# Adjacent score groups, column halves of the second query/key chunk, and sums in another tiling, in a two-layer attention and gated-MLP kernel on one core

## The chip, the cores and the metric

One core of one Trainium2 chip runs the whole program. The metric is the device time of one execution in microseconds (us), quoted as the median of the fast runs. A ratio of two kernels is the mean time of the one kernel's fast runs over the mean of the other's from the same rounds, so it is not quite the ratio of the medians.

## The reference

The sequence has 2048 tokens of width 512. Two attention blocks and two gated-MLP blocks alternate. The changed part is the attention block. It goes through 64 segments of 32 tokens one after the other. Each segment puts 8 memory rows in front, projects q, k and v for 32 heads of 128, and attends over the 40 rows. The first 8 rows of its output are the memory of the next segment, so the segments form a serial chain.

```python
n_seg = S // seg_len                       # 2048 / 32 = 64
mask = (idx[:, None] < M) | (idx[:, None] >= idx[None, :])
mem = mem0
for s in range(n_seg):
    h = jnp.concatenate([mem, xs], axis=1)             # 8 + 32 rows
    q = jnp.einsum('btd,dhe->bhte', h, Wq)             # k, v likewise
    scores = jnp.where(mask, jnp.einsum('bhqe,bhke->bhqk', q, k) * scale, -1e9)
    o = jnp.einsum('bhte,hed->btd', einsum('bhqk,bhke->bhqe', softmax(scores), v), Wo)
    mem = o[:, :M, :]
    outs.append(o[:, M:, :])
# ... x = x + attention(layernorm(x)); x = x + gated_mlp(layernorm(x)); both twice
```

## The kernel before

TensorE does one segment as a fixed stream of stages: q0, k0, q1, k1 (the two chunks of q and k), scores of group 0, v0, a filler, scores of group 1, v1, a filler, the sums of the memory rows (psM), the product with v (psO), the other sums (psD), a filler, the output projection (pw), a filler. The fillers are pieces of work that does not depend on the running segment (keys and values of the next block of rows, "psb", or a late part of the output projection, "pwB"). They cover the time in which VectorE and ScalarE work on the memory rows.

A projection chunk is 16 matmuls of 512 columns, in four column groups of 32. Each matmul carries its own weight load. `halved` says how many of the 16 are issued as two matmuls of 256 columns: the same columns, in more instructions.

```python
PE_PAGE = 256
SEGMENT_PE = 600
FILL_AHEAD = ((0, 0, 0, 106), (0, 0, 0, 94))
# ... cut
def mm_chunk(ps, lhs, rhs, kts=range(KT), halved=0):
    for kt in kts:
        for cg in range(4):
            k, r = 4 * kt + cg, rhs(kt, cg)
            n = halved * (k + 1) // 16 - halved * k // 16
            # ... n: this matmul in two parts of 256 columns, else one of 512
            for a, (o, r) in enumerate(parts):
                nc.tensor.matmul(o, lhsT=lhs(kt, cg), rhs=r, ..., tile_position=(0, 32 * cg))
# ... cut
def fills_of(s):                     # instructions (matmuls and weight loads) of the four fillers
    # ...
    if s % 4 == 0:
        return (2, 2, 4, 8) if s // 4 > 3 else (0, 0, 0, 0)
    return (8, 8, 16, 32) if s // 4 + 1 < NB else (0, 0, 0, 0)

def pads_of(s):                      # how many matmuls of each chunk are halved
    n = (3 * PE_PAGE - SEGMENT_PE - fills_of(s - 1)[3] - sum(fills_of(s)[:3]) + 1) // 2
    pads = dict.fromkeys(("q0", "k0", "q1", "k1", "v0", "v1"), 0)
    for chunk, most in (("v0", 16), ("k1", 16), ("v1", 16 if s % 4 == 0 else 8), ("q1", 12), ...):
        k = min(n, most - pads[chunk])
        pads[chunk] += k
        n -= k
    assert n == 0
    return pads
# ... cut: the order of one segment
r0 = qk(0); r2 = qk(2); qk_T(0, r0); r1 = qk(1); qk_T(2, r2); r3 = qk(3); qk_T(1, r1)
psS = att.tile([P, 2, 512], F32, name="psS")
scores(0)
qk_T(3, r3)
v_mm(0, psV[0][:, 0, :]); fill(); close(0)
scores(1); close(1)
v_mm(1, psV[1][:, 0, :]); fill()
# ... psM from onesG over 128 rows, pv(0), pv(1), psD, fill, Ln and Exp of psM, pw, fill
```

`pads_of` keeps every segment at 3 * 256 = 768 TensorE instructions, matmuls and weight loads counted together. It does so by issuing columns in more instructions than they need.

The softmax here doesn't subtract the row's maximum and nothing guards it: scores larger than these inputs give would overflow.

## Time and profile before

| | us |
|---|---|
| time, median of 3 runs | 1853.05 (1849.69 to 1855.57) |
| the two attention blocks, first to last q0 | 721.3 and 718.8 |
| one segment with a key/value filler, most of them | 11.16 |
| TensorE busy, VectorE busy, ScalarE busy | 1749.7, 1155.0, 1111.5 |

Two more lines of the same profile belong here. The first is from the page's table of DMA queues; its columns are packets, megabytes and the share of 16 engines' time.

```profile
q8 instruction: 400, 6.55, 1.5%
```

The page calls the kind of this queue "instruction". A packet is 6.55 MB / 400 = 16 KiB. TensorE has 51,152 matmuls and 51,176 weight loads, together 102,328, and 102,328 / 400 = 255.8. From these counts I take the packets for TensorE's instructions in pages of 256. They come during the whole of block 0, one every 3.81 us on average.

The second is from the waits of the weight loads (what was waited for: us in all, times, longest).

```profile
PEld L544 <- issue: 27.5, 59, 4.3
```

"issue" is idle time for which the profile shows no semaphore that was waited for. L544 is the matmul of the projection chunks.

### The profile page before, as it was taken

The numbers are of one execution on the slowest core, as the hardware profiler recorded it, in microseconds if no ns is written. First come the engines' busy times: TensorE is split into PE (matmuls) and PEld (weight loads), VectorE is DVE, ScalarE is ACT, GpSimd is POOL, SyncE is SP. The second block draws the span as 40 slices with busy tenths as digits, with TensorE's granted clock in tenths as the row PEclk, the third lists the DMA queues.
The fourth block names the chain that finished last, engine by engine and source line by source line (L and its number), as shares of the span: only waits on it lengthen the run. The fifth ranks groups of instructions, "written<-read, shape, count | busy, mean of one in ns | idle before, by whom it ended". The sixth has DMA issues, their size and how long they took to land.

```text
span 1848.6 us, 109448 instructions
## 1 busy us (share of the span) xinstructions
PE 1749.7 (95%) x51152; PEld 1246.7 (67%) x51176; DVE 1155.0 (62%) x2700; ACT 1111.5 (60%) x2074; POOL 137.1 (7%) x289
## 2 busy tenths in 40 slices
PE   2999999999999999889989999999999999998898
PEld 1777777777777777645547777777777777775455
DVE  1666666677667766584346666666766676665622
ACT  1667777767777766471036667677776777665500
POOL 5000000000000000032010000000000000003000
PEclk8999999999999999999999999999999999999999
DMA  9100000021002111268940000001200121125585
GB/s 347 54 20 19 20 20 21 21 71 41 20 20 82 35 30 34 88 157 172 201 134 22 23 22 22 22 22 45 82 25 23 48 86 26 35 62 150 113 174 131
DMA packets 189327, 126.78 MB, mean 69 GB/s; under 512 B 135896, under 2 KB 164328, under 8 KB 188872
## 3 DMA queue, kind: packets, MB, share of 16 engines
q1 hardware_dynamic: 167016, 71.01, 16.6%
q0 software_dynamic: 10560, 34.07, 5.6%
q10 hardware_dynamic: 11296, 14.70, 2.7%
q8 instruction: 400, 6.55, 1.5%
q14 instruction: 55, 0.45, 0.1%
HBM read 59.29 MB, written 33.56 MB: 50 GB/s over the span
## 4 chain that ended last, share of the span: by engine, by line
PE 86%; DMA 4%; DVE 4%; issue 3%; ACT 2%; POOL 1%; SPq 0%; ACTq 0%; POOLq 0%; DVEq 0%
PE psm L544 24%; PE psV L544 13%; PE pw L599 12%; PE psb L544 10%; PE pg L332 7%; PE psS L722 5%; PE psO L745 4%; PE pwB L611 3%; PE py L360 2%; PE psD L797 2%; PE pz L266 1%; PE psM L787 1%; DMA uT<-u 1%; DMA Wo_sb<-in_A_Wo_dram 1%; PE psM L788 1%
## 5 line engine op out<-in xcount | busy, mean ns | idle before, releaser
L544 PEld LDWEIGHTS <-hA 128*32 128x32 bf16 x19868 | 542.2, 96 | 167.7 <-DVE hA L655 51.6
L701 ACT CAST rows<-psm 128x512 bf16<-128x512 f32 x512 | 300.2, 586 | 197.8 <-PE psm L544 197.8
L544 PE MATMUL psm<-Wq_sb,hA 128*32 128x256 bf16 (+1 forms) x5768 | 274.4, 319 | 11.2 <-DVE hA L655 9.5
L599 PEld LDWEIGHTS <-uT 128*32 128x32 bf16 x16640 | 236.1, 97 | 59.9 <-DVE uT L807 49.8
L599 PE MATMUL pw<-Wo_sb,uT 128*32 128x128 bf16 x16640 | 262.5, 220 | 14.6 <-DVE uT L807 6.3
L544 PE MATMUL psm<-Wk_sb,hA 128*32 128x256 bf16 (+1 forms) x6623 | 275.0, 298 | 1.4 <-issue 0.7
L544 PE MATMUL psV<-Wv_sb,hA 128*32 128x256 bf16 x7477 | 274.7, 284 | 1.1 <-issue 1.0
L705 DVE STREAM_TRANSPOSE QQ<-rows 128x512 bf16<-128x512 bf16 x256 | 182.0, 711 | 77.9 <-ACT rows L701 76.7
L726 ACT ACTIVATE E<-psS 128x448 bf16<-128x448 f32 x256 | 140.0, 547 | 121.8 <-PE psS L722 121.8
L757 DVE TENSOR_TENSOR uT<-psO,Rt 128x384 bf16<-128x384 f32 x256 | 138.6, 541 | 119.3 <-ACT Rt L813 119.0
L705 DVE STREAM_TRANSPOSE KA<-rows 128x512 bf16<-128x512 bf16 x256 | 181.7, 710 | 43.5 <-ACT rows L701 43.2
L807 DVE TENSOR_TENSOR uT<-psO,Rm 128x128 bf16<-128x128 f32 x256 | 62.5, 286 | 169.5 <-PE psD L797 169.5
L813 ACT ACTIVATE Rt<-Rt 128x512 f32<-128x512 f32 x256 | 157.4, 629 | 4.1
L332 PE MATMUL pg<-z2n,wspT 128*128 128x344 bf16 x1024 | 156.1, 311 | 1.0 <-DVE u L340 1.0
L332 PEld LDWEIGHTS <-wspT 128*128 128x128 bf16 x1024 | 98.4, 98 | 55.4 <-issue 8.2
L805 ACT ACTIVATE Rt<-psD 128x1024 f32<-128x1024 f32 x128 | 131.2, 1025 | 6.0
L544 PEld LDWEIGHTS <-hB 128*32 128x32 bf16 x3072 | 88.4, 97 | 68.4 <-DVE hB L559 25.2
L722 PEld LDWEIGHTS <-KA 128*64 128x64 bf16 x2048 | 79.8, 113 | 67.1 <-DVE KA L705 40.4
L729 DVE TENSOR_TENSOR E<-E,maskN 128x448 bf16<-128x448 bf16 x256 | 95.2, 372 | 45.7 <-ACT E L726 45.7
L544 PE MATMUL psb<-Wq_sb,hB 128*32 128x512 bf16 x1024 | 92.1, 390 | 26.2 <-DVE hB L559 26.2
L782 ACT CAST VA<-psV 128x512 bf16<-128x512 f32 x128 | 75.0, 586 | 62.7 <-PE psV L544 62.7
L722 PE MATMUL psS<-QQ,KA 128*64 128x80 bf16 x2048 | 110.1, 208 | 1.9 <-issue 0.9
(147 smaller groups left out, 2219.4 us busy)
## 6 DMA issues: line engine op xcount, KB each, us to landing
Wo_sb<-in_A_Wo_dram POOLq DMA_DIRECT2D x8, 1024.0 KB, 13.5
xs<-xd ACTq DMA_DIRECT2D x32, 256.0 KB
o_d<-o_sb SPq DMA_DIRECT2D x126, 64.0 KB
y_o<-o_d SPq DMA_DIRECT2D x24, 256.0 KB
xd<-y_o SPq DMA_DIRECT2D x22, 256.0 KB
Wq_sb<-in_A_Wq_dram POOLq DMA_DIRECT2D x8, 512.0 KB, 7.2
Wk_sb<-in_A_Wk_dram POOLq DMA_DIRECT2D x8, 512.0 KB, 11.1
Wv_sb<-in_A_Wv_dram POOLq DMA_DIRECT2D x8, 512.0 KB, 11.5
```

What stands on the lines that cost most here:

```text
L332: nc.tensor.matmul(pg[t][:, k, 0:344], lhsT=wsp[t][:, st, :], rhs=z2n[:, st, 344 * k:344 * k + 344], start=(st == 0), stop=(st == NT - 1))
L544: nc.tensor.matmul(o, lhsT=lhs(kt, cg), rhs=r, start=(kt == 0 and a == 0), stop=(kt == KT - 1 or halved > 0), tile_position=(0, 32 * cg), ...
L599: nc.tensor.matmul(po[32 * cg:32 * cg + 32, 0:128], lhsT=lhs[:, n, :], rhs=wo_rhs(h, cg), start=(h == 0), stop=(h == H - 1), tile_position ...
L701: nc.scalar.copy(r[:], ps[:])
L705: nc.vector.transpose(out=QQ[:, j % 2, :, 0:32] if j < 2 else KA[:, j % 2], in_=r[:])
L722: nc.tensor.matmul(pS[64 * g:64 * g + 64, i, c0:80 if K is KA else 112], lhsT=K[:, r, n:n + 2, :].rearrange("p h k -> p (h k)"), rhs=q if ...
L726: nc.scalar.activation(out=E[:, r], in_=pS, func=ACT.Exp, scale=scale)
L729: nc.vector.tensor_tensor(out=E[:, r], in0=E[:, r], in1=maskN[:, j4, :].unsqueeze(1).to_broadcast([P, 4, 112]), op=ALU.mult)
L757: nc.vector.tensor_tensor(out=hview(uT_nxt[:], r, 8, 32), in0=oview(r, 8, 32), in1=Rr[:, :, :, 0:24], op=ALU.mult)
L782: nc.scalar.copy(VA[:, 1].rearrange("p i e -> p (i e)"), psV[1][:, 0, :])
L805: nc.scalar.activation(out=Rt[:], in_=psD[:], func=ACT.Ln)
L813: nc.scalar.activation(out=rt, in_=rt, func=ACT.Exp, scale=-1.0)
```

## The change

The intent is to take changes of tiling and waits out of a segment. The scores of both groups go next to each other. The second chunk of q and of k is computed in two column halves, each in a bank (a buffer that matmuls write into) of its own, so that its copies and transposes can start earlier. The memory-row sums use the tiling of the product with v that follows. The late part of the output projection, used as a filler, is issued in column groups so that it has the tiling of its neighbours. `pads_of` is rewritten too: the halves put 2 x 16 = 32 more matmuls into a segment, and as many are taken out of the other chunks, so a segment keeps its 768 instructions.

```diff
@@ wo_last (the late part of the output projection, a filler)
+            w = P // parts
             for h in heads:
-                nc.tensor.matmul(pwB[:], lhsT=oBs[G][:, n, :], rhs=..., start=..., stop=...)
+                for t in range(0, P, w):
+                    nc.tensor.matmul(pwB[t:t + w, :], lhsT=oBs[G][:, n, t:t + w], rhs=..., tile_position=(0, t))
@@ fills_of
-                return (2, 2, 4, 8) if s // 4 > 3 else (0, 0, 0, 0)
+                return (8, 8, 16, 32) if s // 4 > 3 else (0, 0, 0, 0)
@@ pads_of
-            pads = dict.fromkeys(("q0", "k0", "q1", "k1", "v0", "v1"), 0)
-            for chunk, most in (("v0", 16), ("k1", 16), ("v1", 16 if s % 4 == 0 else 8), ("q1", 12), ("k0", 8), ...):
+            pads = dict(q0=0, k0=0, q1=16, k1=16, v0=0, v1=0)
+            n -= 32
+            for chunk, most in (("k0", 8), ("v0", 8), ("v1", 8), ("v0", 16), ("k0", 16), ("v1", 16), ("q0", 16)):
@@ segment
+            def qk_halves(j):
+                r = rowp.tile([P, 512], BF16, name="rows", tag="rowsQK", bufs=4)
+                for a in range(2):
+                    ps = ((att, attO[1]), (attO[0], accB))[j // 2][a].tile([P, 512], F32, name="psm2")
+                    # 16 matmuls of 256 columns into ps[:, 0:256]
+                    nc.scalar.copy(r[:, 256 * a:256 * a + 256], ps[:, 0:256])
+                    yield
+                    nc.vector.transpose(out=out, in_=r[:, 256 * a:256 * a + 256])
 ...
-            r1 = qk(1)
             qk_T(2, r2)
-            r3 = qk(3)
-            qk_T(1, r1)
-            scores(0)
-            qk_T(3, r3)
-            v_mm(0, psV[0][:, 0, :])
+            q1, k1 = qk_halves(1), qk_halves(3)
+            for g in (q1, q1, k1, q1, k1, k1):
+                next(g, None)
+            v_mm(0, psV)
+            pS = [scores(r) for r in range(2)]
+            # exps and masks of both groups
+            v_mm(1, psW)
             fill()
-            scores(1)
-            v_mm(1, psV[1][:, 0, :])
             fill()
 ...
-            for g in range(2):
-                o = psM[:, 128 * g:128 * g + 128]
-                nc.tensor.matmul(o, lhsT=onesG[:, g, :], rhs=a_part(0, P, 0, 2, 0, 8), ...)
-                nc.tensor.matmul(o, lhsT=onesG[:, g, :], rhs=b_part(0, P, 0, 2, 0, 8), ...)
+            for part in (a_part, b_part):
+                for g in range(2):
+                    nc.tensor.matmul(psM[:, g, 0:128], lhsT=ones[64 * g:64 * g + 64, :],
+                                     rhs=part(64 * g, 64 * g + 64, 0, 2, 0, 8), ...)
             pv(0)
-            pv(1)
             # ... psD
+            # Ln and Exp of psM
+            psO.append(attO[1].tile([P, 2, 512], F32, name="psO"))     # psM's banks
+            pv(1)
             fill()
```

Cut here: the second filler of a segment gets another bank, and the multiplication of the last rows moves behind the transpose that feeds the next segment.

More of the change, by code (lines that the diff above doesn't have):

```diff
@@ L573, in b_units @@
             for k, j in enumerate((0, 2, 1, 3, 4, 5)):
-                ps = (accA if k % 2 == 0 or not early else accB).tile([P, 512], F32, name="psb")
+                if early or k % 2 == 0:
+                    ps = (accA if k % 2 == 0 else accB).tile([P, 512], F32, name="psb")[:]
+                else:
+                    ps = att.tile([P, 512], F32, name="psb2")[:]
                 for kts in (((0,), (1,), (2, 3)), ((0, 1, 2, 3),))[k % 2]:
@@ L582, in out @@
                     if j >= 4:
-                        nc.scalar.copy(bs["VB"][:, j - 4].rearrange("p i e -> p (i e)"), ps[:])
+                        nc.scalar.copy(bs["VB"][:, j - 4].rearrange("p i e -> p (i e)"), ps)
                         return
                     r = rowp.tile([P, 512], BF16, name="rowsB", bufs=2)
-                    nc.scalar.copy(r[:], ps[:])
+                    nc.scalar.copy(r[:], ps)
                     turns.append(lambda: nc.vector.transpose(
@@ L605, in store_last, with wo_last @@
             eng.dma_start(o_d[M + 512 * G:M + 512 * G + 512, :].rearrange("(j r) d -> j r d", r=32)[:, 24:32, :], yB.pop(G)[:])
-        def wo_last(G, heads, pwB):
+        def wo_last(G, heads, pwB, parts=1):
+            w = P // parts
             for h in heads:
                 n = h // 8 * 8 + 2 * (h % 4) + h // 4 % 2
-                nc.tensor.matmul(pwB[:], lhsT=oBs[G][:, n, :], rhs=Wo_sb[:, h, :].rearrange("p (kt g el) -> p g kt el", kt=4, g=4),
-                                 start=(h == heads[0]), stop=(h == heads[-1]))
+                for t in range(0, P, w):
+                    nc.tensor.matmul(pwB[t:t + w, :], lhsT=oBs[G][:, n, t:t + w], rhs=Wo_sb[:, h, :].rearrange("p (kt g el) -> p g kt el", kt=4, g=4),
+                                     start=(h == heads[0]), stop=(h == heads[-1]), tile_position=(0, t))
                 yield
@@ L617, in y_part @@
             pwB = accA.tile([P, DM], F32, name="pwB")
-            for k, _ in enumerate(wo_last(G, range(8 * q, 8 * q + 8), pwB)):
+            for k, _ in enumerate(wo_last(G, range(8 * q, 8 * q + 8), pwB, 4)):
                 if k in (0, 1, 3):
@@ L673, in pads_of @@
             n = (3 * PE_PAGE - SEGMENT_PE - fills_of(s - 1)[3] - sum(fills_of(s)[:3]) + 1) // 2
-            pads = dict.fromkeys(("q0", "k0", "q1", "k1", "v0", "v1"), 0)
-            for chunk, most in (("v0", 16), ("k1", 16), ("v1", 16 if s % 4 == 0 else 8), ("q1", 12), ("k0", 8), ("q1", 16), ("v1", 16),
-                                ("k0", 16), ("q0", 16)):
+            pads = dict(q0=0, k0=0, q1=16, k1=16, v0=0, v1=0)
+            n -= 32
+            for chunk, most in (("k0", 8), ("v0", 8), ("v1", 8), ("v0", 16), ("k0", 16), ("v1", 16), ("q0", 16)):
                 k = min(n, most - pads[chunk])
@@ L705, in qk_T @@
                 nc.vector.transpose(out=QQ[:, j % 2, :, 0:32] if j < 2 else KA[:, j % 2], in_=r[:])
+            def qk_halves(j):
+                r = rowp.tile([P, 512], BF16, name="rows", tag="rowsQK", bufs=4)
+                for a in range(2):
+                    ps = ((att, attO[1]), (attO[0], accB))[j // 2][a].tile([P, 512], F32, name="psm2")
+                    for kt in range(KT):
+                        for cg in range(4):
+                            nc.tensor.matmul(ps[32 * cg:32 * cg + 32, 0:256].rearrange("p (i c) -> p i c", i=2), lhsT=hA_cur[:, kt, :],
+                                             rhs=qk_rhs(j, kt, cg)[:, 2 * a:2 * a + 2], start=(kt == 0), stop=(kt == KT - 1),
+                                             tile_position=(0, 32 * cg))
+                    nc.scalar.copy(r[:, 256 * a:256 * a + 256], ps[:, 0:256])
+                    yield
+                    out = (QQ[:, 1, :, 0:32] if j < 2 else KA[:, 1])[:, 8 * a:8 * a + 8]
+                    nc.vector.transpose(out=out, in_=r[:, 256 * a:256 * a + 256])
             def v_mm(r, ps):
@@ L714, in scores @@
             def scores(r):
-                pS = psS[:, r, 0:448].rearrange("p (i c) -> p i c", i=4)
+                psS = (att, attO[0])[r].tile([P, 512], F32, name="psS")
+                pS = psS[:, 0:448].rearrange("p (i c) -> p i c", i=4)
                 for i in range(4):
@@ L725, in scores, with exps @@
                                              start=(i == 0 and K is KA), stop=True, tile_position=(0, 64 * g), skip_group_check=True)
+                return pS
+            def exps(r, pS):
                 nc.scalar.activation(out=E[:, r], in_=pS, func=ACT.Exp, scale=scale)
@@ L753, in hview, with r_view, last_out @@
                 return t.rearrange("p (b n) q -> p b n q", b=4)[:, 2 * r:2 * r + 2, :, lo:hi]
+            def r_view(r):
+                return Rt[:].rearrange("p g (r n q) -> p g r n q", r=2, n=8)[:, :, r]
             def tok_out(r):
-                Rr = Rt[:].rearrange("p g (r n q) -> p g r n q", r=2, n=8)[:, :, r]
                 nc.vector.tensor_tensor(out=hview(uT_nxt[:], r, 8, 32), in0=oview(r, 8, 32),
-                                        in1=Rr[:, :, :, 0:24], op=ALU.mult)
+                                        in1=r_view(r)[:, :, :, 0:24], op=ALU.mult)
+            def last_out(r):
                 nc.vector.tensor_tensor(out=hview(oB, r, 8 * (s % 16), 8 * (s % 16) + 8), in0=oview(r, 32, 40),
-                                        in1=Rr[:, :, :, 24:32], op=ALU.mult)
+                                        in1=r_view(r)[:, :, :, 24:32], op=ALU.mult)
             r0 = qk(0)
@@ L764, in segment @@
             qk_T(0, r0)
-            r1 = qk(1)
             qk_T(2, r2)
-            r3 = qk(3)
-            qk_T(1, r1)
-            psS = att.tile([P, 2, 512], F32, name="psS")
-            scores(0)
-            qk_T(3, r3)
-            psV = [attO[r].tile([P, 2, 512], F32, name="psV") for r in range(2)]
-            v_mm(0, psV[0][:, 0, :])
-            fill()
-            close(0)
-            nc.vector.tensor_copy(VA[:, 0].rearrange("p i e -> p (i e)"), psV[0][:, 0, :])
-            scores(1)
@@ L778, in segment @@
-            close(1)
-            spare1()
-            v_mm(1, psV[1][:, 0, :])
-            fill()
-            nc.scalar.copy(VA[:, 1].rearrange("p i e -> p (i e)"), psV[1][:, 0, :])
-            psM = accB.tile([P, 512], F32, name="psM")
-            for g in range(2):
-                o = psM[:, 128 * g:128 * g + 128]
-                nc.tensor.matmul(o, lhsT=onesG[:, g, :], rhs=a_part(0, P, 0, 2, 0, 8), start=(g == 0), stop=True, skip_group_check=True)
-                nc.tensor.matmul(o, lhsT=onesG[:, g, :], rhs=b_part(0, P, 0, 2, 0, 8), start=False, stop=True, skip_group_check=True)
@@ L789, in segment @@
-            psO = [attO[r].tile([P, 2, 512], F32, name="psO") for r in range(2)]
+            q1, k1 = qk_halves(1), qk_halves(3)
+            for g in (q1, q1, k1, q1, k1, k1):
+                next(g, None)
+            psV = attO[1].tile([P, 512], F32, name="psV")
+            v_mm(0, psV)
+            nc.vector.tensor_copy(VA[:, 0].rearrange("p i e -> p (i e)"), psV[:])
+            pS = [scores(r) for r in range(2)]
+            for r in range(2):
+                exps(r, pS[r])
+            for r in range(2):
+                close(r)
@@ new lines, in segment @@
+            spare1()
+            psW = accB.tile([P, 512], F32, name="psV")
+            v_mm(1, psW)
+            fill()
+            fill()
+            nc.scalar.copy(VA[:, 1].rearrange("p i e -> p (i e)"), psW[:])
+            psM = attO[1].tile([P, 2, 512], F32, name="psM")
+            for part in (a_part, b_part):
+                for g in range(2):
+                    nc.tensor.matmul(psM[:, g, 0:128], lhsT=ones[64 * g:64 * g + 64, :], rhs=part(64 * g, 64 * g + 64, 0, 2, 0, 8),
+                                     start=(part is a_part), stop=True, skip_group_check=True)
@@ L790, in segment @@
+            psO = [attO[0].tile([P, 2, 512], F32, name="psO")]
             psD = att.tile([P, 2, 512], F32, name="psD")
             pv(0)
-            pv(1)
             for part, q0, q1, c0 in ((a_part, 8, 40, 0), (b_part, 8, 16, 24)):
@@ L798, in segment @@
                                          start=(part is a_part and r == 0), stop=True, skip_group_check=True)
+            Rm = segp.tile([P, 2, 2, 64], F32, name="Rm", bufs=1)
+            rm = Rm[:].rearrange("p g r c -> p g (r c)")
+            nc.scalar.activation(out=rm, in_=psM[:, :, 0:128], func=ACT.Ln)
+            nc.scalar.activation(out=rm, in_=rm, func=ACT.Exp, scale=-1.0)
+            psO.append(attO[1].tile([P, 2, 512], F32, name="psO"))
+            pv(1)
             fill()
-            Rm = segp.tile([P, 2, 2, 64], F32, name="Rm", bufs=1)
-            rm = Rm[:].rearrange("p g r c -> p (g r c)")
-            nc.scalar.activation(out=rm, in_=psM[:, 0:256], func=ACT.Ln)
-            nc.scalar.activation(out=rm, in_=rm, func=ACT.Exp, scale=-1.0)
             Rt = segp.tile([P, 2, 512], F32, name="Rt", bufs=1)
@@ L819, in segment @@
                 build_hA(s + 1, pw)
+            last_out(0)
             if s > 0:
@@ L825, in segment @@
             tok_out(1)
+            last_out(1)
             run(turns)
```

## The prediction

> **What bounds the kernel now.** The page comes first: busy shares, then the chain that ended last. They say TensorE.
>
> ```profile
> PE 1749.7 (95%) x51152; PEld 1246.7 (67%) x51176; DVE 1155.0 (62%) x2700; ACT 1111.5 (60%) x2074; POOL 137.1 (7%) x289
> ...
> PE 86%; DMA 4%; DVE 4%; issue 3%; ACT 2%; POOL 1%; SPq 0%; ACTq 0%; POOLq 0%; DVEq 0%
> ```
>
> A busy share of 95% does not say that every microsecond is matmul streaming[...]. So I read the timeline of one attention segment, TensorE alone; columns are start, time until the group's end, engine, line, operation, tiles, count. There are 128 such segments (64 in each of two attention blocks), in about 1430 of the 1849 us.
>
> ```profile
> 304.74 1.05 PE L544 MATMUL psm<-Wq_sb,hA 128*32 128x512 bf16 x16
> ...
> 307.34 1.07 PE L544 MATMUL psm<-Wk_sb,hA 128*32 128x256 bf16 x32
> 308.34 0.23 PE L722 MATMUL psS<-QQ,KA 128*64 128x80 bf16 x2
> ...
> 308.72 1.07 PE L544 MATMUL psV<-Wv_sb,hA 128*32 128x256 bf16 x32
> 309.60 0.40 PE L544 MATMUL psb<-Wv_sb,hB 128*32 128x512 bf16 x4
> 309.93 0.23 PE L722 MATMUL psS<-QQ,KA 128*64 128x80 bf16 x2
> ...
> 310.30 1.06 PE L544 MATMUL psV<-Wv_sb,hA 128*32 128x512 bf16 x24
> 311.18 0.40 PE L544 MATMUL psb<-Wv_sb,hB 128*32 128x512 bf16 x4
> 311.51 0.23 PE L787 MATMUL psM<-E,onesG 128*128 128x128 bf16 x1
> ...
> 311.84 0.21 PE L745 MATMUL psO<-E,VA 64*128 64x80 bf16 x2
> ...
> 312.35 0.44 PE L797 MATMUL psD<-E,ones 64*128 64x256 bf16 x8
> 312.71 0.62 PE L544 MATMUL psb<-Wv_sb,hB 128*32 128x512 bf16 x8
> 313.16 1.97 PE L599 MATMUL pw<-Wo_sb,uT 128*32 128x128 bf16 x128
> 315.04 1.05 PE L544 MATMUL psb<-Wv_sb,hB 128*32 128x512 bf16 x16
> 315.89 0.39 PE L544 MATMUL psm<-Wq_sb,hA 128*32 128x512 bf16 x1
> ```
>
> One segment is 315.89 - 304.74 = 11.16 us, and stage by stage the same in nearly all segments with a key/value filler. The field 128*32 (64*128, 128*64, 128*128) is the rows and columns of the array used. A projection chunk (16 matmuls of 512, four column groups) streams in 0.866 us if the next stage uses the same tiling (psV at 308.72 to psb at 309.60 is 0.88). **Each change of tiling costs about 0.1 us:** k1 to scores is 1.00 - 0.87 = 0.13; a filler quarter (a fourth of a chunk, 0.216) to scores 0.33 - 0.22 = 0.11; scores 0.375 against eight pairs at 0.0365, 0.08; again 0.08 in the second group; filler to psM 0.335 - 0.22 = 0.12; psM 0.33 - 4 x 0.056 = 0.105; psD 0.367 - 0.276 = 0.09. Seven changes: 0.70 us a segment, 90 us in all. Nothing else idles there much. The waits behind it are just covered:
>
> ```profile
> 310.42 0.55 ACT L726 ACTIVATE E<-psS 128x448 bf16<-128x448 f32 x1 [0.92 <-PE psS L722]
> 311.00 0.39 DVE L729 TENSOR_TENSOR E<-E,maskN 128x448 bf16<-128x448 bf16 x1 [0.32 <-ACT E L726]
> 311.95 0.38 ACT L802 ACTIVATE Rm<-psM 128x256 f32<-128x256 f32 x1
> 312.36 0.42 ACT L803 ACTIVATE Rm<-Rm 128x256 f32<-128x256 f32 x1
> 312.81 0.49 DVE L807 TENSOR_TENSOR uT<-psO,Rm 128x128 bf16<-128x128 f32 x2 [1.42 <-PE psD L797]
> 314.42 0.57 ACT L583 CAST front<-psb 128x512 bf16<-128x512 f32 x1
> ```
>
> The mask ends at 311.39 and psM starts at 311.51; uT's first half is done at about 313.10 and pw starts at 313.16; the copy of the filler ends at 314.99 and the next filler, which takes the same bank, starts at 315.04.
>
> [...] psD's pairs run together (8 matmuls in 0.276 us of streaming, half of what one after the other would take). [...]
>
> **The change part by part.** (T is the time from the start of q0; before, wo (pw) starts at T = 8.42.)
>
> 1. Scores adjacent, after v0: the order is q0 k0 q1a q1b k1a k1b v0 S0 S1 v1 filler filler psM. Tiling changes: v0 to S0 0.12, S1 to v1 0.08, filler to psM 0.11. The two that lay between S0 and S1 go, and v1's follows once.
> 2. Sums on 64 rows with psO's tiling, each group in its own bank: psM to psO no longer changes tiling (-0.105), and its four matmuls run in two pairs, 0.224 to 0.112 us. Changes now 0.12 + 0.08 + 0.11 + 0.09 (last psO to filler) = 0.40. So parts 1 and 2 take 0.30 + 0.11 = **0.41 us** of TensorE time out of a segment.
> 3. Given back: the second half of psO lies in psM's banks, so it waits for Ln of psM. From psM's start: last matmul +0.06, its end +0.22, ScalarE +0.05, Ln 0.385 and +0.05 make 0.76; the stream in front of it (psM 0.12, first psO 0.25, psD 0.28) is 0.65. Exposed: **0.11 us**.
> 4. Column halves of q1 and k1: TensorE time does not change (chunks were largely split into 256-column matmuls already, the count per segment stays 768 instructions with weight loads). ScalarE copies of 256 columns: from 586 ns at 512 and 266 at 128, 0.833 ns a column, so 373; VectorE transposes from 711 and 311, so 444. Adds 4 x 373 - 2 x 586 = 0.32 us to ScalarE and 4 x 444 - 2 x 711 = 0.35 us to VectorE per segment, 41 and 45 us in all, beside TensorE. What it buys is time: k0's copy ends at T = 2.56, then VectorE transposes k0 (to 3.30), q1a, q1b, k1a, k1b at some 0.38 apart: k1a is ready by 4.4, k1b by 4.8. S0 starts at 4.45, S1 at 4.74, its second half at 4.89. Just covered.
> 5. E: S1's last matmul ends at 5.2, two exps back to back end at about 5.95, the second mask at 6.35. psM can start in the stream at 4.45 + 0.67 + 0.87 + 0.43 + 0.11 = 6.53. Covered by 0.1.
> 6. Then psO second half at 7.29, filler 7.63, wo 8.08. uT: Ln ends 7.24, Exp 7.67, uT's first half 7.99: covered by a hair.
> 7. Second filler of a segment in another bank: 0.08 us of waiting goes at 315.04. But the path wo, predicated copy (0.28), transpose (0.31), q0 becomes the limit; with last_out moved behind it, about 0.04 is won.
>
> Filler segments: 0.41 - 0.11 + 0.04 = 0.34; as two waits are covered by a hair I take 0.32. There are 92: 29 us. **Wo filler in column groups:** 24 segments now have that filler with the full array, their period is 11.50 against 11.16, by more tiling changes (v0 to pwB, pwB to wo, wo to pwB, pwB to q0). With parts of 32 columns the stream time stays (four at once) and the 0.34 goes too: 24 x 0.66 = 16 us. **Segments without filler** (12, about 11.5 us) are bound by latency: S1 ends about 0.6 us sooner, all of which reaches psM and wo: 7 us, of which I count 5. The b blocks (some 400 us) are not touched. Sum: 29 + 16 + 5 = 50 us; 1853 - 50 = 1803.
>
> **The rivals.** (a) A new wait takes it: k1b's transpose, the mask or uT lands 0.1 to 0.2 us late in every segment. For: all three are covered by 0.1 or less, and VectorE gets longer in front of S1; segments with two filler transposes delay q0's transpose to T = 1.9. Against: k0's transpose still waits for ScalarE's copy at 2.56, so that delay is absorbed. Time: 1816 to 1828. (b) VectorE or ScalarE becomes the bound. A segment has 7.96 to 8.47 us of each in the windows I summed; with 0.35 more that is at most 8.8 of 10.84. Against it; if true the period stays near 11.1, 1845. (c) Transfers take it back: sums that wait for loaded rows (12.9 us over 6 waits) wait longer when segments shorten. At most a few us. (d) All is covered and psO's wait is smaller than I think: 0.4 a segment, 1790.
>
> **Range and chances.** Centre 1803. (a) in half its size gives the upper end, 1824; (d) with more from the segments without filler gives 1786. The 2% line is at 1816; I need 0.24 us a segment in the filler segments to pass it along with the rest. Faster by over 2%: 0.80; within: 0.18; slower: 0.02.
>
> **What would show it right or wrong.** Filler segments near 10.84 us from q0 to q0, those with Wo filler the same within 0.05; S0 and S1 together 0.67 us; psM to psO 0.11 to 0.14; a stop of about 0.11 before the second psO with ScalarE's Rm as releaser; VectorE's busy total near 1200 and ScalarE's near 1152 us. Wrong: TensorE waits for KA (line of the scores' weights) in the middle of S1, or for E ahead of psM, or for uT ahead of wo, of over 0.1 us in most segments; or stages of matmuls that stream slower than before in the column groups of the Wo filler.

## The result, and the profile after

| | before | after |
|---|---|---|
| median, us (4 runs each, same chip) | 1853.61 (1849.69 to 1855.57) | 1839.51 (1835.55 to 1843.14) |
| attention block 0 and 1, first to last q0 | 721.3, 718.8 | 712.4, 718.7 |

The ratio is 0.9926, with a 95% interval of 0.9897 to 0.9955. That is 14 us faster by the medians. 50 us were predicted, and 1839.51 lies above the range. The first block gained 8.9 us, the second 0.1.

The page's first lines, busy times and the chain that ended last:

```profile
PE 1729.5 (94%) x51154; PEld 1277.5 (69%) x51178; DVE 1172.4 (64%) x2956; ACT 1130.6 (61%) x2330; POOL 136.6 (7%) x289
...
PE 87%; issue 4%; DMA 3%; DVE 3%; ACT 1%; POOL 1%; SPq 0%; ACTq 0%; POOLq 0%; DVEq 0%
```

TensorE is still the bound. It is busy for 20 us less, but the span shrank by only 8.6 (1848.6 to 1840.0). "issue" is 4% of the chain; it was 3%. The number of TensorE instructions did not change, and the instruction queue again has 400 packets. The waits of the weight loads, and below them those of the matmuls, say where the rest went:

```profile
PEld L544 <- issue: 62.5, 166, 4.2
...
PEld L602 <- issue: 16.5, 40, 2.8
```

```profile
PE psm L544 <- issue: 8.9, 27, 0.8
...
PE pw L602 <- issue: 8.1, 19, 2.6
```

Waiting for "issue" ahead of the projections' weight loads went from 27.5 us in 59 places to 62.5 us in 166. Before, the other three were 8.4 us in 18 (weight loads of pw), 1.0 in 2 (psm) and 4.4 in 5 (pw). One wait for another engine grew as much: the weight load of psM waits for the mask (E, from VectorE) for 44.5 us in 105 places, where it was 4.5 in 13. It is hidden behind the matmuls still running: the matmuls of psM themselves wait for E for 0.5 us in 2 places, and from the last filler matmul to psM it is 0.31 us in the median segment, before and after. The timeline of one segment, TensorE alone (start, time to the group's end, engine, line, operation, tiles, count, idle before):

```profile
303.75 1.06 PE L719 MATMUL psm<-Wq_sb,hA 128*32 128x256 bf16 x32
304.62 1.06 PE L719 MATMUL psm<-Wk_sb,hA 128*32 128x256 bf16 x32
305.49 1.06 PE L544 MATMUL psV<-Wv_sb,hA 128*32 128x512 bf16 x24
306.49 0.23 PE L743 MATMUL psS<-QQ,KA 128*64 128x80 bf16 x2
...
307.13 1.44 PE L544 MATMUL psV<-Wv_sb,hA 128*32 128x512 bf16 x18
...
308.97 0.29 PE L815 MATMUL psM<-E,ones 64*128 64x128 bf16 x4
309.09 0.20 PE L769 MATMUL psO<-E,VA 64*128 64x80 bf16 x2
...
309.34 0.44 PE L824 MATMUL psD<-E,ones 64*128 64x256 bf16 x8
309.73 0.21 PE L769 MATMUL psO<-E,VA 64*128 64x80 bf16 x2
...
310.07 0.62 PE L544 MATMUL psb<-Wv_sb,hB 128*32 128x512 bf16 x8
310.51 2.08 PE L602 MATMUL pw<-Wo_sb,uT 128*32 128x128 bf16 x128
312.38 1.08 PE L544 MATMUL psb<-Wv_sb,hB 128*32 128x512 bf16 x16
313.32 1.05 PE L544 MATMUL psm<-Wq_sb,hA 128*32 128x512 bf16 x16
314.19 0.83 PE L544 MATMUL psm<-Wk_sb,hA 128*32 128x512 bf16 x18
315.31 0.41 PE L544 MATMUL psm<-Wk_sb,hA 128*32 128x512 bf16 x6 [0.29 <-issue]
```

The wins are all there. The two score groups take 307.13 - 306.49 = 0.64 us together, psM to psO is 0.12, and psD to the second psO is 0.39. But k0 (from 314.19) stops in its middle for "issue", and the 18 matmuls of v1 from 307.13 on take 1.44 us to the group's end, where the chunks before them take 1.06. Nothing that these matmuls read or write had changed in between.

The trace's records of the instruction queue lie over these stops. Each row is one page of 256 instructions. The last two columns are the first matmul of the page and the matmul before it. They come from laying the trace over the program's list of instructions.

```
page fetched (us)      matmul before   first matmul of the page
305.08 to 305.96       307.14          307.55   in v1    (0.4 apart)
308.67 to 309.96       311.19          311.30   in pw    (0.1 apart)
312.49 to 313.87       314.75          315.31   in k0    (0.6 apart)
317.03 to 317.95       318.92          319.33   in v1    (0.4 apart)
```

Every stop in these rows sits at the first instruction of a page. Counting the weight loads of the whole block gives the same: 74 of block 0 start over 0.3 us after the one before without a semaphore to wait for, and 67 of these have the same place in a count by 128, that is, one page of 128 matmuls and 128 loads. The page's fetch ended 1.3 to 1.6 us before that instruction, and the fetch of the page after it began 1.1 to 1.7 us after it. In all of block 0 no fetch of a next page began less than 0.5 us after the first instruction of the page before it.

This gave **theory S (supply)**, an assumption made from the distances below: TensorE cannot go from one page of 256 instructions to the next in less than about 3.75 us. (As a floor for every page this does not hold; see e5.) Where two stops follow each other directly, the pages lie 3.73 to 3.75, 4.00 to 4.03 or 4.28 us apart (26 cases in block 0). By the theory a segment of three pages then cannot be shorter than 3 x 3.75 = 11.25 us on average. Before, the stream of a segment was 11.16 us, 3.72 a page, just at that limit. After, it is 10.79 us (8 of the 90 segments with a key/value filler, those without stops; their median is 11.23), 3.60 a page, below it. The idle time at page boundaries, over what the matmul before them needs and counted where it is above 0.15 us, sums to 9.9 us in both blocks before and to 42.8 after.

The **rival, theory D (dependence)**: the stops are short waits for data or banks that the profile files under "issue", and they come with the new order of the stages. A second rival is contention: the fetches are slow because other transfers are in the way.

### The profile page after: what moved, and what is told of

It reads as the page before. It is cut to its first block, busy times and chain, and to the rows that moved or that the text cites.

```text
span 1840.0 us, 109962 instructions
## 1 busy us (share of the span) xinstructions
PE 1729.5 (94%) x51154; PEld 1277.5 (69%) x51178; DVE 1172.4 (64%) x2956; ACT 1130.6 (61%) x2330; POOL 136.6 (7%) x289
## 4 chain that ended last, share of the span: by engine, by line
PE 87%; issue 4%; DMA 3%; DVE 3%; ACT 1%; POOL 1%; SPq 0%; ACTq 0%; POOLq 0%; DVEq 0%
PE psm L544 13%; PE pw L602 13%; PE psV L544 13%; PE psm L719 12%; PE psb L544 10%; PE pg L332 8%; PE psS L743 4%; PE psO L769 4%; PE pwB L616 3%; PE py L360 3%; PE psD L824 2%; PE psM L815 1%; PE pz L266 1%; DMA Wo_sb<-in_A_Wo_dram 1%; DMA uT<-u 1%
## 5 line engine op out<-in xcount | busy, mean ns | idle before, releaser
L544 PEld LDWEIGHTS <-hA 128*32 128x32 bf16 x11102 | 361.5, 96 | 165.2 <-DVE hA L660 53.4
L544 PE MATMUL psV<-Wv_sb,hA 128*32 128x256 bf16 (+1 forms) x5880 | 288.1, 315 | 0.6 <-issue 0.2
L602 PEld LDWEIGHTS <-uT 128*32 128x32 bf16 x16640 | 238.6, 97 | 61.6 <-DVE uT L836 42.5
L706 ACT CAST rows<-psm 128x512 bf16<-128x512 f32 x256 | 149.8, 585 | 146.8 <-PE psm L544 146.8
L719 PEld LDWEIGHTS <-hA 128*32 128x32 bf16 x8192 | 237.8, 97 | 1.3 <-issue 0.5
L722 ACT CAST rows<-psm 128x256 bf16<-128x256 f32 x512 | 191.2, 374 | 17.6 <-PE psm L719 0.3
L750 ACT ACTIVATE E<-psS 128x448 bf16<-128x448 f32 x256 | 126.3, 541 | 117.2 <-PE psS L743 117.2
L836 DVE TENSOR_TENSOR uT<-psO,Rm 128x128 bf16<-128x128 f32 x256 | 62.5, 286 | 174.8 <-PE psO L769 174.8
L544 PE MATMUL psm<-Wk_sb,hA 128*32 128x256 bf16 (+1 forms) x3158 | 151.9, 308 | 10.3 <-issue 8.9
L544 PE MATMUL psm<-Wq_sb,hA 128*32 128x512 bf16 x2064 | 135.8, 384 | 10.2 <-DVE hA L660 8.8
L719 PE MATMUL psm<-Wq_sb,hA 128*32 128x256 bf16 x4096 | 138.5, 273 | 0.0
L719 PE MATMUL psm<-Wk_sb,hA 128*32 128x256 bf16 x4096 | 138.0, 273 | 0.0
L710 DVE STREAM_TRANSPOSE QQ<-rows 128x512 bf16<-128x512 bf16 x128 | 88.9, 695 | 45.5 <-ACT rows L706 45.5
L710 DVE STREAM_TRANSPOSE KA<-rows 128x512 bf16<-128x512 bf16 x128 | 90.6, 708 | 38.3 <-ACT rows L706 37.8
```

The source lines that it names most:

```text
L544: nc.tensor.matmul(o, lhsT=lhs(kt, cg), rhs=r, start=(kt == 0 and a == 0), stop=(kt == KT - 1 or halved > 0), tile_position=(0, 32 * cg), ...
L602: nc.tensor.matmul(po[32 * cg:32 * cg + 32, 0:128], lhsT=lhs[:, n, :], rhs=wo_rhs(h, cg), start=(h == 0), stop=(h == H - 1), tile_position ...
L706: nc.scalar.copy(r[:], ps[:])
L710: nc.vector.transpose(out=QQ[:, j % 2, :, 0:32] if j < 2 else KA[:, j % 2], in_=r[:])
L719: nc.tensor.matmul(ps[32 * cg:32 * cg + 32, 0:256].rearrange("p (i c) -> p i c", i=2), lhsT=hA_cur[:, kt, :], rhs=qk_rhs(j, kt, cg)[:, 2 * ...
L722: nc.scalar.copy(r[:, 256 * a:256 * a + 256], ps[:, 0:256])
```

## The experiments

All twelve kernels gave the right result. Sets 1, 2 and 3 are the three chips.

| run | set | before, same set (us) | this (us) | ratio, 95% interval | mean fetch of a page in the blocks (us) |
|---|---|---|---|---|---|
| after, first result | – | 1853.61 | 1839.51 | 0.9926 (0.9897–0.9955) | 1.14 |
| e1_after_dense | 1 | 1849.79 | 1975.74 | 1.0681 (1.0621–1.0741) | 1.08, 1.13 |
| e2_before_dense | 1 | 1849.79 | 1969.69 | 1.0629 (1.0572–1.0686) | 1.08, 1.14 |
| e3_after_lean | 1 | 1849.79 | 1837.98 | 0.9919 (0.9870–0.9969) | 1.13, 1.12 |
| e4_after_q1whole | 1 | 1849.79 | 1835.93 | 0.9928 (0.9871–0.9986) | 1.13, 1.12 |
| e5_after_shift | 2 | 1837.05 | 1853.28 | 1.0087 (1.0070–1.0104) | 1.06, 1.05 |
| e6_after_oldsum | 2 | 1837.05 | 1811.14 | 0.9853 (0.9833–0.9873) | 1.06, 1.08 |
| e7_after_wo1 | 2 | 1837.05 | 1811.83 | 0.9849 (0.9827–0.9871) | 1.04, 1.07 |
| e8_after_planned | 2 | 1837.05 | 1809.72 | 0.9843 (0.9828–0.9859) | 1.08, 1.06 |
| e9_after_again | 3 | 1846.12 | 1823.51 | 0.9862 (0.9819–0.9905) | 1.05, 1.06 |
| e10_oldsum_again | 3 | 1846.12 | 1825.57 | 0.9880 (0.9838–0.9922) | 1.08, 1.07 |
| e11_wo1_again | 3 | 1846.12 | 1832.50 | 0.9916 (0.9882–0.9950) | 1.07, 1.08 |
| e12_planned_again | 3 | 1846.12 | 1814.76 | 0.9823 (0.9787–0.9859) | 1.10, 1.07 |

### e1_after_dense and e2_before_dense: more instructions, the same columns

Every projection matmul of 512 columns of the running segment is issued as two of 256; the fillers stay whole. A filler segment has 856 instructions in place of 768. Columns, data, banks and waits stay the same. The same edit went into the kernel after (e1) and the kernel before (e2).

```diff
 def pads_of(s):
-            assert n == 0
-            return pads
+            return dict.fromkeys(pads, 16)
```

> The changed kernel with every projection chunk split into 256-column matmuls, so 856 instead of 768 TensorE instructions in a segment with filler (matmuls and weight loads together), the same columns streamed, the same waits. Theory S (supply): TensorE's instructions arrive in pages of 256, and a page needs about 3.73 us from one page boundary to the next (3.6 to 4.0 between stalled boundaries in the changed kernel's trace). Then 856/256 x 3.73 = 12.5 us a segment in place of 11.2 to 11.3, and the kernel takes about 1975 us (1940 to 2010). Theory D (dependency: the new stops are waits for data or banks, such as k0's bank or the accumulator of the filler): the instruction count does not matter, 1840 us within 15.

> The kernel before with every projection chunk split in the same way: 856 instructions in a segment with key/value filler. Theory S: it runs at the pace of its pages too, about 12.5 us a segment in place of 11.16, near 1970 us (1935 to 2005), within 1.5% of the changed kernel with as many instructions although its stream of matmuls is 50 us longer. Theory D: no change, 1853 within 15, and slower than the changed kernel with the same splits by the 14 us they differ by now.

Measured: 1975.74 and 1969.69 us. Theory S had said 1975 and 1970, theory D 1840 and 1853. That S hit both within 1 us is luck: the four runs of each spread over 17 and 15 us. The instruction queue of each page, e1 first:

```profile
q8 instruction: 441, 7.23, 1.5%
```

```profile
q8 instruction: 436, 7.14, 1.5%
```

41 and 36 pages more than the 400 of each original cost 126 and 120 us over the kernel before of the same set. The starts of the fetches lie 3.73 and 3.76 us apart on average in the two blocks of e1, and about 3.78 in those of e2. For weight loads, "issue" is now the largest wait of e1:

```profile
PEld L544 <- issue: 104.5, 146, 4.4
PEld L602 <- issue: 85.2, 95, 2.0
```

So at these counts the number of instructions sets the time, and it does so in the kernel before as well. The two kernels, 14 us apart at 768 instructions, are 6 us apart the other way round at this count (the intervals overlap), where e1 has five pages more (its filler of the output projection has more instructions): with pages 3.73 to 3.78 us apart on average, the stages saved no longer show. Theory D falls. A limit on each single instruction is no rival either: pw passes 256 instructions in 1.79 us, 7 ns each, where it does not stop. Contention does not explain these two runs either: fetches took 1.08 to 1.14 us on average here and 1.14 in the first profile after, so they were not slower where the kernel was.

### e3_after_lean and e4_after_q1whole: fewer instructions

e3 drops all the padding (728 instructions a filler segment). e4 also computes q1 whole again, in the bank that the scores use later (696).

```diff
 def pads_of(s):
-            assert n == 0
-            return pads
+            return dict.fromkeys(pads, 0)
```

```diff
 # e4, besides:
-            q1, k1 = qk_halves(1), qk_halves(3)
-            for g in (q1, q1, k1, q1, k1, k1):
-                next(g, None)
+            r1, k1 = qk(1), qk_halves(3)      # q1 in the bank "att"
+            next(k1)
+            qk_T(1, r1)
+            for g in (k1, k1):
+                next(g, None)
```

> The changed kernel without the splits that only pad a segment to three pages: 728 instructions in place of 768, and page boundaries drift through the segment. Theory S: 2.84 pages a segment instead of 3, so pages are slack on average, but some boundaries fall into the dense stretch around wo; I estimate 0.1 to 0.2 us a segment less, 1815 to 1835 us, and the stops are no longer at one place in k0. Theory D: 1840 within 5, the stop in k0 stays.

> As the lean one, and the second query chunk whole again (16 matmuls of 512 in place of 32 of 256): 696 instructions. VectorE's last half transpose of the second key chunk should end at the same time, as it waits for the transposes before it. Theory S: 2.72 pages a segment, 1810 to 1832 us, no slower than the lean one. Theory D: as the lean one, 1840, or slower by up to 0.1 us a segment (13 us) if the halves of q1 mattered.

Both missed their expectation by a few us: 1837.98 and 1835.93, no more than the change itself. By the time alone theory D (1840, within 5 for e3) did better here; against it stands that the stops in k0 all but went (65 above 0.25 us in the kernel after, 3 in e3). Pages were no longer short on average: they are 4.03 to 4.21 us apart, in 377 and 361 pages. In e3 the stop went elsewhere. Waits of the matmuls and of the weight loads of e3:

```profile
PE pw L602 <- issue: 34.9, 47, 1.6
```

```profile
PEld L602 <- issue: 45.1, 51, 2.4
```

The output projection pw is 128 matmuls with 128 weight loads, 256 instructions in 1.79 us (its length in the kernel after where it does not stop). Without the padding the page boundaries drift through the segment, and where one page lies mostly in pw, it is used up in little more than those 1.79 us, by estimate, while the pages of e3 and e4 lie 4.03 to 4.21 us apart on average. The matmuls of pw wait on "issue" 47 times in e3, 34.9 us in all. e4 shows the same: laid over its list of instructions, its trace has 49 stops in pw, 46 us in all. So the average is not enough: **the stops come page by page; in e3 and e4 they came in the dense stretch pw.** The padding of the kernel before does two things: it costs instructions, and it keeps the boundaries in fixed places, where they cost 9.9 us in both blocks.

### e5_after_shift: the same instructions, boundaries elsewhere

In block 0 the filler ahead of the first segment is counted as 42 instead of 106 instructions. `pads_of` then adds 60 instructions to the first segment (30 matmuls and 30 weight loads), and all page boundaries behind it, in both blocks, move 60 instructions earlier in the stages.

```diff
-FILL_AHEAD = ((0, 0, 0, 106), (0, 0, 0, 94))
+FILL_AHEAD = ((0, 0, 0, 42), (0, 0, 0, 94))
```

> The changed kernel with 60 more TensorE instructions in the first segment of the first block alone (30 splits more), so that in all later segments the page boundaries fall about 60 instructions earlier in the code, in the first matmuls of q0, in the scores and early in wo, instead of in k0, v1 and wo; nothing else differs. Theory S (instruction supply): the stops in k0 go and others appear at the new places, the time stays, 1840 within 10. Theory D (data or a bank is late for k0): the stops in k0 stay where they are.

Timeline of e5, from the filler after pw into the next segment, and the largest wait of its matmuls:

```profile
304.66 1.04 PE L544 MATMUL psb<-Wk_sb,hB 128*32 128x512 bf16 x16
305.58 0.40 PE L544 MATMUL psm<-Wq_sb,hA 128*32 128x512 bf16 x4
306.23 0.83 PE L544 MATMUL psm<-Wq_sb,hA 128*32 128x512 bf16 x12 [0.24 <-issue]
306.87 1.06 PE L544 MATMUL psm<-Wk_sb,hA 128*32 128x512 bf16 x24
```

```profile
PE psm L544 <- issue: 55.9, 116, 1.2
```

The stop moved from k0 into q0, where theory S put it, and k0 passes without one. The fifth matmul of q0 waits for the same data as the fourth, so no dependence explains it. The time missed: 1853.28 was expected to be near 1840, and it is 16 us above the kernel before of its set, on a chip where the change's variants gain 25. There are 112 such stops in q0 in the two blocks, of about 0.67 us each: the page that ends in q0 now contains most of pw and the filler behind it, which pass in some 2.7 us. A shift of 60 instructions thus costs more than the whole change wins on this chip.

The same stops correct theory S. From its first weight load to that of the next page, a page that ends in such a stop took 3.4 us in the median, 86 of 117 less than 3.5, and the shortest 3.1. So 3.75 us is the least that a page took between two stops in block 0 of the first profile, and about the mean of all pages in e1 and e2, where the supply was the limit most of the time; it is no floor for a single page. e1 has distances of 3.5 us even between two stops. Why a page comes sooner after one that began without a stop is not shown here.

### e6_after_oldsum and e7_after_wo1: the change without one of its parts

e6 has the old sums on 128 rows (a change of tiling more per segment). e7 has the old filler of the output projection on the full array.

```diff
 # e6
-            for part in (a_part, b_part):
-                for g in range(2):
-                    nc.tensor.matmul(psM[:, g, 0:128], lhsT=ones[64 * g:64 * g + 64, :], rhs=part(64 * g, 64 * g + 64, 0, 2, 0, 8), ...)
+            for g in range(2):
+                o = psM[:, 0, 128 * g:128 * g + 128]
+                nc.tensor.matmul(o, lhsT=onesG[:, g, :], rhs=a_part(0, P, 0, 2, 0, 8), ...)
+                nc.tensor.matmul(o, lhsT=onesG[:, g, :], rhs=b_part(0, P, 0, 2, 0, 8), ...)
 # e7
-            ... enumerate(wo_last(G, range(8 * q, 8 * q + 8), pwB, 4))
+            ... enumerate(wo_last(G, range(8 * q, 8 * q + 8), pwB))
-                return (8, 8, 16, 32) if s // 4 > 3 else (0, 0, 0, 0)
+                return (2, 2, 4, 8) if s // 4 > 3 else (0, 0, 0, 0)
```

> The changed kernel with the sums as before (K = 128 with the zero-padded ones, one bank), the rest unchanged, 768 instructions. It adds 0.1 us of tiling change and 0.1 us of stream to each of 128 segments, 27 us of TensorE work. If the stream is the bound, 1867 us. Theory S: most of it lies where the pages would have stopped TensorE anyway, 1840 to 1850 us, ratio to the changed kernel's below 1.006.

> The changed kernel with the Wo filler on the full array again (8 matmuls a segment in place of 32 narrow ones, as many instructions by padding). Stream as the bound: the 24 segments take 0.34 us more each, 8 us, 1848 us. Theory S: their stream of 10.79 + 0.34 = 11.13 us is still under three pages of 3.75 us, so 0 to 4 us more.

Measured 1811.14 and 1811.83, each 25 to 26 us under the kernel before of the set, and far under the 1840 to 1867 that had been expected from the first chip. Each has a part of the change undone, and yet almost twice the gain of the first result. This chip fetched a page faster: 1.04 to 1.08 us on average, against 1.14. The fetches of e6 and e7 follow each other at 3.67 to 3.74 us, and 29 of the 63 segment periods of e7 in block 0 lie at 10.79 or 10.80 us (3.60 a page, often two or three in a row), close to the length that the prediction had worked out. In set 2 the kernel after itself did not run, so these two could not say what their part was worth. That is why set 3 repeats them beside it.

### e8_after_planned: padding laid out per segment

If S holds, a version should win that has few instructions and keeps page boundaries out of bad places. e8 takes e4 (q1 whole, 696 instructions) and replaces `pads_of` by a table. The table was computed so that few pages fall mostly into pw: per segment, how many matmuls of q0, k0, v0 and v1 are halved.

```diff
+PLAN = [[...64 rows of (q0, k0, v0, v1)...], [...]]      # one list per attention block
 def pads_of(s):
-            return dict.fromkeys(pads, 0)
+            return PLAN[not first][s]
```

> The kernel with q1 whole (697 instructions at least in a filler segment) and a number of splits chosen for each segment so that few page boundaries fall where 256 instructions pass in less than 3.75 us. Theory S: my hand calculation of boundaries with 3.77 us a page gives 23 us of stops in each attention block in place of 33, so about 1820 us (1808 to 1835), the fastest so far. Theory D: no effect, 1836 as e4.

Measured 1809.72, inside the expected range and below its middle, with 376 pages. It is 27 us under the kernel before of its set, and the fastest of the set by a little. Its ratio, 0.9843, cannot be told from 0.9853 and 0.9849 of e6 and e7, which have no plan, so what the plan is worth is not shown here.

### e9 to e12: the kernel after, and three versions, on a third chip

The four kernels are the one after, e6, e7 and e8, unchanged and beside each other.

> The changed kernel itself. In the second set of runs the kernel before took 1837 us in place of 1850 to 1853 and its instruction pages were fetched in 1.06 us in place of 1.13 (means of DMA queue q8), so that was another chip. Theory S: the time of the changed kernel depends on how fast the pages come. On a chip with the kernel before near 1837 us and fetches of 1.06 us, segments run at the stream's 10.8 us and the time is near 1800 us (1792 to 1812), ratio about 0.98; on one with the kernel before near 1851 us and fetches of 1.13 us it is again 1840 us, ratio 0.993. Theory D: the ratio is 0.993 on either.

> The changed kernel with the sums as before, on the same chip as the changed kernel. With fetches of 1.06 us: 1811 us as before, some 10 us above the changed kernel. With fetches of 1.13 us: within 8 us of the changed kernel, 1838 to 1848, although TensorE has 27 us more to do.

> The changed kernel with the Wo filler on the full array, on the same chip as the changed kernel. With fetches of 1.06 us: 8 us above the changed kernel, its stream. With fetches of 1.13 us: 0 to 4 us above it.

> The kernel with fewer instructions and splits placed per segment, on the same chip as the changed kernel. With fetches of 1.13 us: 1822 us (1810 to 1832), 10 to 25 us below the changed kernel. With fetches of 1.06 us: 1810 us, no better than the changed kernel.

The kernel after reached 1823.51 (1812.49 to 1830.81) here, 22.6 us under the kernel before by the medians, where the first result had 14. The waits of the weight loads of e9:

```profile
PEld L544 <- issue: 45.1, 120, 5.6
```

That is 120 waits on "issue" against 166 in the first profile, with a mean fetch of 1.05 to 1.06 us against 1.14. The idle time at page boundaries, counted as above, is 29.0 us against 42.8. The same program on two chips differs in how long it waits for its instructions.

The expectation had two cases, by the mean fetch, and neither came true: the fetches are as short as in the fast case, yet the kernel before took 1846 us and e9 lies outside 1792 to 1812. e10 missed in the same way (1811 expected), and e12, expected no better than the changed kernel, came out 9 us under it with overlapping ranges. The mean fetch does not tell the chips apart: e7 and e11 are the same program, fetched in 1.04 and 1.07 us and in 1.07 and 1.08, but they took 1811.83 and 1832.50 us.

e10's segments without stops take 10.90 us in place of 10.79: the old sums cost 0.11 us a segment, 14 us in 128 segments. Yet its time, 1825.57, is only 2 us above e9's, and both spread over 18 us: the 14 us do not show in full. That waits for the next page hide the rest is a guess that no run here shows. e11 is 9 us above e9; the 24 segments with a filler of the output projection take 11.62 us on average instead of 11.14, which makes 11.5, but the intervals of the two overlap, so this is a hint and no proof. e12 is the fastest of its set, as e8 was: 1814.76, 31 us under the kernel before and 9 under the kernel after by the medians, though the ranges of those two runs overlap (1811.82 to 1820.41, 1812.49 to 1830.81). Against the kernel before, its ratio is 0.9823.

## Why the prediction was wrong, point by point

1. **The bound.** TensorE as the bound was right. What was read from the view was too narrow: the stream of matmuls was taken to be the limit. The supply of instructions lay right beside it (3.72 us a page against about 3.75), and the page showed its traffic in the instruction queue's line (400 packets).
2. **Scores adjacent and sums in the tiling of psO** (0.41 us a segment). Right: scores 0.645 us together in the median segment against 0.67, psM to psO 0.122 against 0.11 to 0.14. The halving was taken from psD before: 4 matmuls of 256 columns and 4 of 64 stream in 0.276 us, and at the pace of psM (0.056 us for 128 columns) the 1280 columns would take 0.56 one after the other, an estimate.
3. **The wait before the second psO** (0.11 us). Right: psD to psO takes 0.392 us against 0.276 of streaming, 0.117 more. The profile names no releaser for it, but in the segment shown the Ln of psM ends at 309.67 and this psO starts at 309.73.
4. **The halves.** ScalarE's copies went from 300.2 us to 191.2 + 149.8 = 341.0, so +41 as worked out; its busy total still rose only to 1130.6, not 1152. In part that is counting: the two exps now follow each other and overlap in the records, so their busy time fell from 140.0 to 126.3 although one takes 541 ns against 547. VectorE's halves took 403 ns, not 444, and its total rose to 1172.4, not 1200. Neither engine became a bound. **The failed step stands in this part, in a half sentence: "the count per segment stays 768 instructions with weight loads". It was taken as a reason why nothing changes.** It is the reason why most segments did not get shorter on the first chip: 768 instructions are three pages, three pages need about 11.25 us when they come at 3.75, and the median filler segment measures 11.23 in place of the predicted 10.84. A lower count alone would not have helped either: e3, with 728, took as long, with its stops elsewhere.
5. **E, uT and the second filler.** No matmul came to wait for the keys, for E or for uT in most segments, so rival (a) did not happen: the weight loads of the scores wait 26.8 us for the keys (40.4 before), those of pw 42.5 for uT (49.8), and the longer wait of psM's weight load for E is hidden, as shown above. The working says "covered by 0.1" for E; its own figures give 6.53 - 6.35 = 0.18. pw ran in 1.79 us where it does not stop, against 1.88 before.
6. **The sum.** Filler segments were predicted at 10.84 us. Those that do not stop measure 10.79 (8 of 90). With the filler of the output projection none of 24 is below 10.96 in the first profile; in e9, the same program, 5 of 24 reach 10.79 to 10.81. As an estimate, 126 periods x (11.16 - 10.79) = 46.6 us of stream gained in the two blocks, near the 50 predicted. The blocks got 9.0 us shorter (1440.1 to 1431.1). 42.8 - 9.9 = 32.9 us of the difference are stops at page boundaries; the remaining 4.7 are not placed. The same account for e9, against the first profile before (another chip): 31.3 us shorter and 19.1 us more at the boundaries, 50.4 together. The sum "1853 - 50" thus had about the right gain in stream and left out the term that took most of it. None of the rivals named it.
7. **Segments without filler** were to bring 5 us. Their periods after are mixed with stops and show no gain that I can separate.

**Shown:** that more instructions at the same columns took longer (e1, e2: 41 and 36 pages more, 126 and 120 us) and that the stops follow the page boundaries (e5: 60 instructions of shift, and 112 stops of about 0.67 us in q0). **In keeping with it, but from differences near the noise or from one chip against another:** that TensorE work added costs little (e10), and that stops are fewer where fetches are shorter (e9; e7 against e11 speaks against it). **Open:** what the 3.75 us consist of apart from the fetch of about 1.1 us, why the distances come in steps of about 0.27 us, and what sets the chips apart, since the mean fetch does not. What the parts of the change are worth alone was not settled either: the ranges of e9, e10 and e11 overlap.

## What to carry to other kernels

Count TensorE's instructions, weight loads included, beside its columns. Where the pages were the limit (e1, e2), every 256 of them took 3.73 to 3.78 us on average, about 15 ns an instruction (3.75 / 256). A stream of matmuls that averages near or under that gained less from less work than its sum promised: 14 us of 50 in the first result. The pace is not the same on every chip: in set 2, 55 of the 90 key/value-filler segments of e7 passed in 10.81 us or less, 3.60 a page. Fewer instructions alone did not help either: e3 and e4, with 377 and 361 pages, took 1837.98 and 1835.93 us, and stopped in the output projection, a dense stretch of short matmuls (256 instructions in 1.79 us). With its boundaries shifted by 60 instructions the changed kernel ended 16 us slower than the kernel before (e5). That long matmuls around a dense stretch would help is the estimate, which e8 and e12 do not settle. A projection matmul issued in two halves took no more streaming time (in the profile after, 0.87 us for a chunk of 16 matmuls of 512 columns, q0 at 313.32, and 0.87 for one of 32 of 256, q1 at 303.75), but 88 instructions more a segment cost about 1 us of it, an estimate from the 126 and 120 us of e1 and e2 over 128 segments. A change of tiling cost 0.08 to 0.13 us in the profile before. In the profile, look at the instruction queue's packets and at "issue" ahead of weight loads before promising that a removed stage shortens the run.
